# A decode layer's W_down tail loaded in two transfers, with TensorE's loop unrotated and the residual added on VectorE

## The chip, the cores and the metric

The kernel runs on one core of one Trainium2 chip. The metric is device time in microseconds (us), from launch to the last byte written. Engines are named as the profile names them: PE (TensorE; PEld is its weight load), DVE (VectorE), ACT (ScalarE), POOL (GpSimd), SP (SyncE, which issues nearly all transfers here). A trailing q (SPq, DVEq) is the engine's instruction queue.

## The reference

One decode step of a transformer layer for two sequences of one token each. Layernorm, attention over a cache of 8192 positions with 32 heads of 128, a residual, and then a gated feed-forward block with a residual:

```python
q = (layernorm(x) @ wq) -> [b, 32, 1, 128]
p = softmax(q . k_cache * 128**-0.5)          # 8192 positions for each (b, head)
h = x + (p . v_cache) @ wo
d = layernorm(h)
gate, up = d @ W_gate, d @ W_up               # 512 -> 1376
y = h + ((gate * (gate > 0)) * up) @ W_down   # 1376 -> 512
```

All inputs are bfloat16. K and V are 134 MB each, so nearly all of the 281 MB that are read is the cache.

## The kernel before

**Tiles.** The 64 combinations of sequence and head are taken as 32 pairs (`NP`), two heads of one sequence to a pair. A pair has one K tile and one V tile of 128 partitions x 128 positions x 128, 4 MB each. Four buffers `slot[0..3]` take them in turn: even pairs use slots 0 (K) and 1 (V), odd pairs slots 2 and 3. SP issues all loads in one queue, in the order K of pair p + 2, then V of pair p + 2 (`load`, L170; L704 to L711), and waits before each until the slot is free: before K until DVE has multiplied the old tile and PE has transposed it (`kf`), before V until PE's PV product of the old tile is done (token `pv`).

**Scores.** Of the 128 positions of each partition, 96 (`JC`) are scored on DVE: multiply by q (`k_mult`, L553), four halving adds (`k_add`, L558), and a reduce of the last 8 (`k_reduce`, L569). The other 32 are scored on PE in `k_part` (L354): transposes through PSUM (L383), ACT copies them out (`evac`, L581), score products (L366). ACT takes the exponentials of both parts (`exp_pe`, `exp_dve`, L508) into `e_t`, with row sums into `zs`.

**PV and what follows.** `pv` (L394) multiplies the exponentials with V: 32 products of 512 columns (L407) add up in PSUM bank `Op[0]`, over two pairs, which make one group g of two heads for both sequences. `sums` (L583) copies the bank to `os_sb`, `collect` (L420) adds its strips into `Ob`, `z_sum` (L433) adds up the row sums, DVE normalises (L516, L519) and scales (`o_scale`, L523). `o_spread` (L528) places the result in `O_l`, `o_gather` (L436) turns it into columns for the product with wo.

**The loops.** Fifteen iterations (`NI`) of two pairs each run as hardware loops on PE (L444), ACT (L622) and DVE (L588); POOL and SP run straight. PE's loop is rotated by one PV: an iteration does `z_sum`, `k_part` of the even pair, PV of the odd pair of the iteration before, `collect`, PV of the even pair, `k_part` of the odd pair, `o_gather` (L445 to L453). The PV of the odd pair stands behind the transposes of the next pair's K. In the first iteration it runs over a slot that holds wq, with exponentials of zero; so `slot_sem[3]` is raised by hand (L341), `zs` is filled with a pattern of ones (L207), and V of pair 1 is loaded only behind that product (L701 to L703).

**The tail.** Pairs 62 (`P0`) and 63 (`P1`) are written out behind the loops. PE (L465 to L488): `z_sum`, `k_part` of 62, PV of 61, `collect`, `o_gather`, the product with the first 30 heads of wo (L476, 30 products), its collection (L482), `k_part` of 63, PV of 62, PV of 63 in two parts, each with its own transfer and semaphore (L487). DVE (L650 to L663): for pair 62 multiply, first add, then wait for `collect` of pair 61 (`t_ob_loop`), normalise, `o_spread`, the other adds and the reduce; then pair 63. SP (L712 to L727) loads V 63 in two parts, and into slot 0, once K 62 has been used, W_up, W_gate and the first 1280 rows of W_down in blocks of 4, 4 and 2 row groups; the last 96 rows go to `wd_last` in one transfer (L727).

**The feed-forward block.** h is gathered in `hb` (L750); its mean is taken off into `d_b` (L757). PE does 44 products with W_up (L777, `ffn_in`), then 16 small products that add h itself into `Op[0]` (L788, the residual), then two for the variance (L803), then 44 with W_gate. DVE takes the inverse variance `r2` for all 128 partitions (L809, L811), multiplies the up part with it into `u_sb` (L814), and forms `hd` = max(gate, 0) * `u_sb` (L820). The W_down products (L829) add to the residual in `Op[0]`, each block behind its semaphore `sem_wd[k]`; the copy at L835 rounds the sum, and two transfers (L839) write it out.

Of the kernel before, what the change touches and what calls it, by code (L numbers as in the profile page):

```python
# [39 lines left out]
def bass_sequential_preLN__gqa_block_cached__glu_gated_reglu__decode_kernel(  # L40
# [33 lines left out]
    WD_BLOCKS = ((0, 4), (4, 4), (8, 2))  # L74

    with ExitStack() as es:
# [22 lines left out]
        sem_wd = [S(f"wd{i}") for i in range(4)]  # L99
# [42 lines left out]
        ve = sb("ve", [128, B], F32)  # L142
        r2 = sb("r2", [128, B], F32)
# [22 lines left out]
        if True:  # L166

            def program():
# [36 lines left out]
                pool.run(nc.gpsimd.memset(zs[:], 0.0))  # L205
                pool.last()
                for a in range(2):  # L207
                    t_const = pool.run(nc.gpsimd.memset(zs[64 * a:64 * a + 64, a:4:2, :], 1.0))
                    pool.last()
# [92 lines left out]
                t_sel = dve.run(nc.vector.tensor_copy(out=rows[:, DR:], in_=rows[:, 0:DR]))  # L302
                nc.sync.dma_start(
# [37 lines left out]
                nc.tensor.sem_inc(slot_sem[3], 16)  # L341
# [52 lines left out]
                def pv(T, p, parts, between=None, done=None):  # L394
                    s = (2 * p + 1) % 4
                    v_t = tile(s)
                    q = p % PG
                    n = 0
                    for j0, j1, waits in parts:
                        if between and n:  # L400
                            nc.tensor.wait_ge(*waits[0])
                            between()
                        for sem, val in waits:
                            nc.tensor.wait_ge(sem, val)
                        for j in range(j0, j1, VJ):
                            c = 32 * (n % 4)
                            i = nc.tensor.matmul(  # L407
                                Op[0][c:c + 16, :], lhsT=e_t[q][:, j // VJ, :],
                                rhs=v_t[:, j:j + VJ, :].rearrange("p j d -> p (j d)"),
                                start=(q == 0 and n < 4), stop=(q == PG - 1 and n >= J // VJ - 4),  # L410
                                skip_group_check=True)
                            if T is body and n == q == 0:
                                T.mark(("fp", p), i)
                            n += 1
                    if done:
                        i.then_inc(done, 1)
                    else:
                        T.mark(("pv", p), i)

                def collect(T, a, done=None):  # L420
                    nc.tensor.wait_ge(a2p, a)
                    for jj in range(VJ):
                        i = nc.tensor.matmul(  # L423
                            Ob[:, 0:4], lhsT=os_sb[:, jj * Dh:(jj + 1) * Dh],
                            rhs=sel[:, 4 * jj:4 * jj + 4], start=(jj == 0), stop=(jj == VJ - 1))
                        if done and jj == 0:
                            T.mark(done, i)
                    if T is body:
                        i.then_inc(p2d, 1)
                    else:  # L430
                        T.mark("ob", i)
# [12 lines left out]
                with nc.Fori(0, NI, engines=OrderedEngineSet([nc.tensor.engine])):  # L444
                    nc.tensor.wait_ge(a2p, 1)  # L445
                    z_sum(Ob)
                    k_part(body, 0, (2, 3, 4, 5), ((k2p, 1),))
                    pv(body, 1, ((JC, J, ((slot_sem[3], 16),)), (0, JC, ())), done=p2a)
                    collect(body, 7, ("pv", 1))
                    pv(body, 0, ((JC, J, ((slot_sem[1], 16), (a2p, 6))), (0, JC, ((a2p, 8),))))  # L450
                    k_part(body, 1, (9, 10, 11, 12), ((k2p, 2),))
                    nc.tensor.wait_ge(l2p, 1)
                    o_gather(body)  # L453
                    nc.tensor.wait_ge(a2p, EV)
                    nc.tensor.sem_inc(l2p, -1)
                    nc.tensor.sem_inc(slot_sem[1], -16)
                    nc.tensor.sem_inc(slot_sem[3], -16)
                    nc.tensor.sem_inc(k2p, -2)
                    nc.tensor.sem_inc(a2p, -EV)
# [5 lines left out]
                nc.tensor.wait_ge(a2p, 1)  # L465
                z_sum(Ob)
                k_part(tail, P0, (2, 3, 4, 5), ((k2p, 1),))
                pv(tail, P0 - 1, ((JC, J, ((slot_sem[3], 16),)), (0, JC, ())))
                collect(tail, 7)
                t_ob_loop = (pe.sem, tail.at["ob"])  # L470
                nc.tensor.wait_ge(l2p, 1)
                o_gather(tail)
                nc.tensor.wait_ge(a2p, 8)
# [11 lines left out]
                k_part(tail, P1, (11, 12, 13, 14), ((k2p, 2),))  # L485
                pv(tail, P0, ((JC, J, ((slot_sem[1], 16), (a2p, 10))), (0, JC, ())))
                pv(tail, P1, ((V_LAST, J, ((sem_vl[0], 16), (a2p, 16))), (0, V_LAST, ((a2p, 16), (sem_vl[1], 16)))),  # L487
# [8 lines left out]
                def tokp(kind, p, *g):  # L496
                    return tok(kind if kind == "og" else (kind, p) + g, (p + (kind == "pv")) // 2)
# [59 lines left out]
                def k_add(w, run):  # L557
                    run(nc.vector.tensor_tensor(  # L558
                        out=prod[:, 0:JC, 0:w], in0=prod[:, 0:JC, 0:w], in1=prod[:, 0:JC, w:2 * w], op=ALU.add))

                def k_adds(p, run, last, w=Dh):
                    while w > 8:
                        w //= 2
                        last()
                        k_add(w, run)
                    last()
# [54 lines left out]
                nc.scalar.sem_inc(a2p, 1)  # L621
                with nc.Fori(0, NI, engines=OrderedEngineSet([nc.scalar.engine])):  # L622
                    n_a = 0
                    for q in range(PG):
# [7 lines left out]
                        if q == 0:  # L632
                            n_a += 1
                            nc.scalar.wait_ge(p2a, n_a)
                            sums()
# [9 lines left out]
                for p in range(NP):  # L645
# [4 lines left out]
                    if p >= P0:  # L650
# [5 lines left out]
                        dve.last()  # L656
                        k_add(Dh // 2, dve.run)
# [4 lines left out]
                        k_adds(p, dve.run, dve.last, Dh // 2)  # L662
                        t_s[p] = dve.run(k_reduce(p))  # L663
# [20 lines left out]
                    if p == P0:  # L684
                        evacs()
                        act.wait(tokp("pv", p - 1))
                        sums()
                        act.wait(tok("og", NI))
                        to_pe(nc.scalar.activation(
                            out=O_all[:].rearrange("p r b -> p b r"),  # L690
                            in_=Op[1][:, 0:B * DR].rearrange("p (b r) -> p b r", r=DR), func=ACT.Copy))
                        act.wait(tok("op", NI))
                        to_pe(nc.scalar.activation(out=os_sb[:], in_=Op[1][:], func=ACT.Copy))
                        act.wait(t_s[p])
                        exp_dve(p)
# [5 lines left out]
                    if p == 0:  # L701
                        sp.wait(tok(("pv", 1), 0))
                        load(3, A_v_cache, 1)  # L703
# [13 lines left out]
                    if p == NP - 2:  # L717
# [9 lines left out]
                        nc.sync.dma_start(wd_last[:], B_W_down[F - FR:]).then_inc(sem_wd[3], 16)  # L727
# [7 lines left out]
                collect(tail, 17)  # L735
# [50 lines left out]
                for k in range(4):  # L786
                    for c in range(DC):
                        nc.tensor.matmul(  # L788
                            Op[0][32 * k:32 * k + B, c:128:DC], lhsT=hb[:, c * B:(c + 1) * B],
                            rhs=ident[:, 32 * k:32 * k + 32], start=(c == 0), stop=False, skip_group_check=True)  # L790
# [10 lines left out]
                pe.wait(t_vh)  # L801
                for k in range(2):
                    i = nc.tensor.matmul(Sp[0][:, 32:32 + B], lhsT=onesn[:], rhs=vh[:, k * B:(k + 1) * B],  # L803
                                         start=(k == 0), stop=(k == 1))
                t_var = pe.run(i)
                pe.wait((sem_w[1], 16))
                t_g = ffn_in(Op[1], wgt, 0, FC)
                dve.wait(t_var)
                dve.run(nc.vector.tensor_scalar_add(out=ve[:], in0=Sp[0][:, 32:32 + B], scalar1=eps))  # L809
                dve.last()  # L810
                dve.run(nc.vector.reciprocal(out=r2[:], in_=ve[:]))  # L811
                dve.last()
                dve.wait(t_u)
                dve.run(nc.vector.tensor_tensor(  # L814
                    out=u_sb[:].rearrange("p (f b) -> p f b", b=B),
                    in0=Sp[1][:, 0:FC * B].rearrange("p (f b) -> p f b", b=B),
                    in1=r2[:].unsqueeze(1).broadcast_to([128, FC, B]), op=ALU.mult))
# [4 lines left out]
                    in1=u_sb[:], op0=ALU.max, op1=ALU.mult))  # L822
                pe.wait(t_hd)
                order = [(f, k) for k, (r0, n) in enumerate(WD_BLOCKS) for f in range(r0, r0 + n)] + [(10, 3)]
                for n, (f, k) in enumerate(order):
                    pe.wait((sem_wd[k], 16))
                    kp = 128 if f < 10 else FR
                    for m in range(4):
# [3 lines left out]
                            start=False, stop=(n == FC - 1), skip_group_check=True)  # L832
                t_y = pe.run(i)
                dve.wait(t_y)
                t = dve.run(nc.vector.tensor_copy(out=o_r, in_=Op[0][:, 0:128]))  # L835
# [38 lines left out]
```

## Time and profile before

| | |
|---|---|
| median of three runs | 662.96 us (662.75 to 663.32) |
| time of the profiled execution | 662.96 us |
| its span, first to last instruction | 661.7 us, so 1.26 around it |
| busy: PE, PEld | 322.2, 193.9 us (49%, 29%) |
| busy: DVE | 469.1 us (71%) |
| busy: ACT, POOL | 213.8, 74.0 us (32%, 11%) |
| moved | 281.17 MB, mean 425 GB/s |
| DVE's longest wait in sum, for K tiles | 141.6 us in 29 waits |
| PE's longest wait in sum, for ACT's exponentials before `z_sum` | 143.6 us in 15 waits |
| mean granted TensorE clock | 0.594 of full speed |

The profile is of one execution. Its page gives busy times, moved bytes in 40 slices of 16.5 us, the chain of work that ended last (followed back from the last instruction), and the costliest groups of instructions. The trace answers for single stretches: the timeline lists instructions in order with start, duration, engine, line and, in brackets, the idle time before them and what ended it; equal neighbours are merged (x8), and matmuls overlap, so a group's time is from its first start to its last end. Time to landing of a transfer counts from its issue. An idle engine costs nothing where another sets the end.

### The profile page before, as it was taken

To read this page: it belongs to the slowest core of one execution; us is meant where nothing else is said; L and a number is where in the kernel's file an instruction comes from. 1 tells how busy PE (TensorE), PEld (TensorE's weight loads), DVE (VectorE), ACT (ScalarE), POOL (GpSimd) and SP (SyncE) were. 2 spreads that over 40 slices of the span, in tenths; PEclk is the share of its full clock that TensorE was granted. 3 is DMA by queue.
4 is the path that set the end of the run, shared out by engine and by line. 5 is a ranking of instruction groups with operands and counts; after the bars stand their busy time and mean duration, and the time that the engine had idled before them with its cause. 6 is when DMAs were issued, how large, how long until landed. Compare 5 with 4: busy or idle time off the path is not lost.

```text
span 661.7 us, 7610 instructions
## 1 busy us (share of the span) xinstructions
PE 322.2 (49%) x3101; PEld 193.9 (29%) x3101; DVE 469.1 (71%) x279; ACT 213.8 (32%) x431; POOL 74.0 (11%) x127
## 2 busy tenths in 40 slices
PE   2760562616455262644517344451736436174777
PEld 0330342214332121423313233321324223142445
DVE  1585576778767678876767877676787767688891
ACT  1622232233343224334322333432334332232330
POOL 3002002020200202020020202002020200202000
PEclk9875555665557566565755575575555756555665
DMA  9999999999999999999999999999999999999995
GB/s 376 431 430 437 430 430 440 422 436 434 424 438 430 432 438 424 436 434 424 438 430 432 436 426 434 434 426 438 430 432 436 424 434 438 424 436 430 433 416 229
DMA packets 10653, 281.17 MB, mean 425 GB/s; under 512 B 1202, under 2 KB 1300, under 8 KB 1812
## 3 DMA queue, kind: packets, MB, share of 16 engines
q1 hardware_dynamic: 10632, 281.06, 98.9%
q8 instruction: 5, 0.08, 0.1%
q14 instruction: 4, 0.03, 0.0%
q10 hardware_dynamic: 12, 0.00, 0.0%
HBM read 281.05 MB, written 0.00 MB: 425 GB/s over the span
## 4 chain that ended last, share of the span: by engine, by line
DMA 76%; DVE 19%; PE 3%; ACT 1%; issue 1%; SPq 0%; DVEq 0%; ACTq 0%
DMA slot<-in_A_k_cache_dram 76%; DVE prod L553 16%; DVE prod L558 3%; PE O L407 1%; PE Ob L423 0%; DVE scores L569 0%; PE T L383 0%; ACT kT L581 0%; PE S L777 0%; PE O L777 0%; PE O L829 0%; ACT e L508 0%; ACT os_sb L584 0%; SPq L171 0%; PE S L366 0%
## 5 line engine op out<-in xcount | busy, mean ns | idle before, releaser
L553 DVE TENSOR_TENSOR prod<-slot,q_c 128x12288 bf16<-128x12288 bf16 x32 | 209.9, 6559 | 148.3 <-DMA slot<-in_A_k_cache_dram 141.6
L558 DVE TENSOR_TENSOR prod<-prod 128x6144 bf16<-128x6144 bf16 (+3 forms) x128 | 212.2, 1658 | 7.8
L581 ACT ACTIVATE kT<-T 128x1024 bf16<-128x1024 bf16 x128 | 126.4, 1022 | 148.1 <-PE T L383 145.1
L383 PE MATMUL T<-ident_f,slot 128*128 128x128 f32 x512 | 117.2, 387 | 66.3 <-DVEq L602 66.3
L407 PE MATMUL O<-slot,e 128*16 128x512 bf16 x1056 | 115.3, 600 | 59.0 <-ACT e L508 58.8
L383 PEld LDWEIGHTS T<-ident_f,slot 128*128 128x128 f32 x512 | 85.3, 200 | 81.3 <-DVEq L602 80.5
L508 ACT ACTIVATE e<-scores 64x96 bf16<-64x96 f32 x64 | 19.5, 304 | 202.4 <-DVEq L616 196.6
L434 PE MATMUL Ob<-zs,ones_f 128*128 128x8 f32 x32 | 9.3, 364 | 143.6 <-ACT e L508 143.6
L550 POOL COPY q_c<-q_all 128x136 bf16<-128x136 bf16 x32 | 57.4, 1794 | 195.1 <-DVEq L606 165.0
L366 PE MATMUL S<-q_c,kT 128*128 128x4 bf16 x1024 | 47.8, 169 | 37.6 <-ACT kT L581 37.0
L407 PEld LDWEIGHTS O<-slot,e 128*16 128x16 bf16 x1056 | 29.4, 117 | 116.5 <-ACT e L508 65.6
L366 PEld LDWEIGHTS S<-q_c,kT 128*128 128x128 bf16 x1024 | 40.4, 105 | 65.5 <-ACT kT L581 64.1
L434 PEld LDWEIGHTS Ob<-zs,ones_f 128*128 128x128 f32 x32 | 7.8, 304 | 145.2 <-ACT e L508 145.1
L533 POOL MEMSET O_l<- 128x40 bf16 (+1 forms) x13 | 1.8, 136 | 304.0 <-DVEq L613 304.0
L569 DVE TENSOR_REDUCE scores<-prod 128x96 f32<-128x768 bf16 x32 | 30.5, 953 | 2.8
L423 PEld LDWEIGHTS Ob<-sel,os_sb 128*128 128x128 f32 x136 | 23.0, 255 | 26.2 <-ACT os_sb L584 26.2
L423 PE MATMUL Ob<-sel,os_sb 128*128 128x4 f32 x136 | 24.4, 303 | 11.9 <-ACT os_sb L584 11.9
L584 ACT ACTIVATE os_sb<-O 128x512 f32<-128x512 f32 x17 | 10.1, 597 | 45.0 <-PE O L407 45.0
L581 ACT ACT_TABLE_LOAD x15 | 19.2, 1283 | 0.3
L508 ACT ACTIVATE e<-S 64x32 bf16<-64x32 f32 x64 | 12.9, 202 | 15.2 <-PE S L366 14.8
L508 ACT ACTIVATION_READ_ACCUMULATOR e<-S 64x1 f32 x64 | 12.8, 201 | 0.7
L508 ACT ACTIVATION_READ_ACCUMULATOR e<-scores 64x1 f32 x64 | 11.8, 184 | 0.0
(104 smaller groups left out, 87.8 us busy)
## 6 DMA issues: line engine op xcount, KB each, us to landing
slot<-in_A_k_cache_dram SPq DMA_DIRECT2D x32, 4096.0 KB, 30.8
slot<-in_A_v_cache_dram SPq DMA_DIRECT2D x31, 4096.0 KB, 29.6
slot<-in_A_wq_dram SPq DMA_DIRECT2D x1, 4096.0 KB, 12.2
X<-in_A_wo_dram SPq DMA_DIRECT2D x1, 3840.0 KB, 50.3
slot<-in_A_v_cache_dram SPq DMA_DIRECT2D x1, 3072.0 KB, 20.5
slot<-in_B_W_up_dram SPq DMA_DIRECT2D x1, 1376.0 KB, 25.5
slot<-in_B_W_gate_dram SPq DMA_DIRECT2D x1, 1376.0 KB, 28.4
slot<-in_A_v_cache_dram SPq DMA_DIRECT2D x1, 1024.0 KB, 22.6
```

What stands on the lines that cost most here:

```text
L366: i = nc.tensor.matmul(Sp[p % 2][:, 2 * jj:2 * jj + 4], lhsT=kv_[:, k, r, :], rhs=q_c[p % 2][:, 4 * r:4 * r + 4], start=(r == 0), stop=(r ...
L383: i = nc.tensor.transpose(Tp[g % 2][:, k * 128:(k + 1) * 128], k_t[:, j:j + 2, :].rearrange("p j d -> p (j d)").bitcast(F32), ident_f[:])
L407: i = nc.tensor.matmul(Op[0][c:c + 16, :], lhsT=e_t[q][:, j // VJ, :], rhs=v_t[:, j:j + VJ, :].rearrange("p j d -> p (j d)"), start=(q == ...
L423: i = nc.tensor.matmul(Ob[:, 0:4], lhsT=os_sb[:, jj * Dh:(jj + 1) * Dh], rhs=sel[:, 4 * jj:4 * jj + 4], start=(jj == 0), stop=(jj == VJ - 1))
L434: return nc.tensor.matmul(bank[:, ZC:ZC + 8], lhsT=ones_f[:], rhs=zs[:], start=True, stop=True)
L508: i = nc.scalar.activation(out=e_t[q][h, j0 // VJ:j1 // VJ, 8 * q:8 * q + 8].rearrange("p g (j a) -> p g j a", a=2)[:, :, :, a], in_=src(h ...
L550: nc.gpsimd.tensor_copy(out=q_c[p % 2][:], in_=q_all[:, p]).then_inc(g2d, 1)
L553: return nc.vector.tensor_tensor(out=prod[:, 0:JC, :], in0=tile((2 * p) % 4)[:, 0:JC, :], in1=q_c[p % 2][:, 8:QW].unsqueeze(1).broadcast_t ...
L558: run(nc.vector.tensor_tensor(out=prod[:, 0:JC, 0:w], in0=prod[:, 0:JC, 0:w], in1=prod[:, 0:JC, w:2 * w], op=ALU.add))
L569: return nc.vector.tensor_reduce(out=scores[p % PG][:, 0:JC], in_=prod[:, 0:JC, 0:8], axis=AX.X, op=ALU.add)
L581: to_pe(nc.scalar.activation(out=kT[gg % 2][:], in_=Tp[gg % 2][:].bitcast(BF16), func=ACT.Copy))
L584: to_pe(nc.scalar.activation(out=os_sb[:], in_=Op[0][:], func=ACT.Copy))
```

## The change

- PE's loop is no longer rotated. An iteration does `k_part` of the even pair, `collect` of the group before, PV of the even pair, `k_part` of the odd pair, `o_gather`, PV of the odd pair (behind its own exponentials), `z_sum`. The dummy product of the first iteration goes, with the raised semaphore, the pattern of ones and ACT's extra increment of `a2p`; ACT no longer waits ahead of `sums` in the loop.
- V of pair 1 is loaded behind the q projection, ahead of `X` (wo), in place of behind the dummy product.
- In the tail, `collect` of pair 61 comes ahead of `k_part` of 62, and DVE normalises that group behind the reduce of pair 62 in place of behind its first add. ACT does `sums` ahead of the tail's first copies, and `exp_dve` of 62 ahead of the second copy to `os_sb`.
- The residual is no longer added in PSUM. The 16 products go to `Tp[0]`, DVE copies them to `h_r`, and the last instruction on DVE is `Op[0] * r2 + h_r` in place of the copy. The inverse variance comes off `u_sb` (now a plain copy) and is made per output row: two variance products ahead of W_gate become eight small ones behind it.
- The last 96 rows of W_down load as 68 and 28 rows with a semaphore each; the last product waits for both.

The diff, cut to its core:

```diff
+    WD_TAIL = ((0, 68), (68, 28))
...
-                for a in range(2):
-                    t_const = pool.run(nc.gpsimd.memset(zs[64 * a:64 * a + 64, a:4:2, :], 1.0))
-                    pool.last()
+                t_const = pool.run(nc.gpsimd.memset(zs[:], 0.0))
...
+                sp.wait(t_q)
+                load(3, A_v_cache, 1)
                 nc.sync.dma_start(
                     X[:], A_wo[0:128 * DR].rearrange("(p r) n -> p (r n)", r=DR)).then_inc(sem_wo, 16)
...
-                nc.tensor.sem_inc(slot_sem[3], 16)
...
                 with nc.Fori(0, NI, engines=OrderedEngineSet([nc.tensor.engine])):
-                    nc.tensor.wait_ge(a2p, 1)
-                    z_sum(Ob)
-                    k_part(body, 0, (2, 3, 4, 5), ((k2p, 1),))
-                    pv(body, 1, ((JC, J, ((slot_sem[3], 16),)), (0, JC, ())), done=p2a)
-                    collect(body, 7, ("pv", 1))
-                    pv(body, 0, ((JC, J, ((slot_sem[1], 16), (a2p, 6))), (0, JC, ((a2p, 8),))))
-                    k_part(body, 1, (9, 10, 11, 12), ((k2p, 2),))
+                    k_part(body, 0, (1, 2, 3, 4), ((k2p, 1),))
+                    collect(body, 6)
+                    pv(body, 0, ((JC, J, ((slot_sem[1], 16), (a2p, 5))), (0, JC, ((a2p, 7),))))
+                    k_part(body, 1, (8, 9, 10, 11), ((k2p, 2),))
                     nc.tensor.wait_ge(l2p, 1)
                     o_gather(body)
-                    nc.tensor.wait_ge(a2p, EV)
                     nc.tensor.sem_inc(l2p, -1)
+                    pv(body, 1, ((JC, J, ((slot_sem[3], 16), (a2p, 12))), (0, JC, ((a2p, EV),))))
+                    z_sum(Ob)
...
-                nc.tensor.wait_ge(a2p, 1)
-                z_sum(Ob)
+                collect(tail, 1)
+                t_ob_loop = (pe.sem, tail.at["ob"])
                 k_part(tail, P0, (2, 3, 4, 5), ((k2p, 1),))
-                pv(tail, P0 - 1, ((JC, J, ((slot_sem[3], 16),)), (0, JC, ())))
-                collect(tail, 7)
-                t_ob_loop = (pe.sem, tail.at["ob"])
...
                         t_dm[p] = dve.run(k_mult(p))
-                        dve.last()
-                        k_add(Dh // 2, dve.run)
+                        k_adds(p, dve.run, dve.last)
+                        if p == P0:
+                            dve.wait(tokp("pv", p - 2))
+                        t_s[p] = dve.run(k_reduce(p))
                         if p == P0:
                             dve.wait(t_ob_loop)
                             normalize(Ob, dve.run, dve.last)
                             o_spread(g - 1, dve, dve.run(o_scale()))
-                        k_adds(p, dve.run, dve.last, Dh // 2)
-                        t_s[p] = dve.run(k_reduce(p))
...
-                    if p == 0:
-                        sp.wait(tok(("pv", 1), 0))
-                        load(3, A_v_cache, 1)
...
-                        nc.sync.dma_start(wd_last[:], B_W_down[F - FR:]).then_inc(sem_wd[3], 16)
+                        for k, (r0, n) in enumerate(WD_TAIL):
+                            nc.sync.dma_start(
+                                wd_last[r0:r0 + n], B_W_down[F - FR + r0:F - FR + r0 + n]).then_inc(sem_wd[3 + k], 16)
...
-                        nc.tensor.matmul(
-                            Op[0][32 * k:32 * k + B, c:128:DC], lhsT=hb[:, c * B:(c + 1) * B],
-                            rhs=ident[:, 32 * k:32 * k + 32], start=(c == 0), stop=False, skip_group_check=True)
+                        i = nc.tensor.matmul(
+                            Tp[0][32 * k:32 * k + B, c:128:DC], lhsT=hb[:, c * B:(c + 1) * B],
+                            rhs=ident[:, 32 * k:32 * k + 32], start=True, stop=True)
+                t_hr = pe.run(i)
+                pe.wait((sem_w[1], 16))
+                t_g = ffn_in(Op[1], wgt, 0, FC)
...
+                pe.wait(t_vh)
+                for m in range(4):
+                    for k in range(2):
+                        i = nc.tensor.matmul(Sp[0][32 * m:32 * m + B, 32:33], lhsT=vh[:, k * B:(k + 1) * B],
+                                             rhs=onesn[:, 0:1], start=(k == 0), stop=(k == 1))
...
-                    pe.wait((sem_wd[k], 16))
+                    pe.wait((sem_wd[k], 16), (sem_wd[max(k, 2 * k - 2)], 16))
...
-                t = dve.run(nc.vector.tensor_copy(out=o_r, in_=Op[0][:, 0:128]))
+                t = dve.run(nc.vector.scalar_tensor_tensor(
+                    out=o_r, in0=Op[0][:, 0:128], scalar=r2[:, 0:1], in1=h_r, op0=ALU.mult, op1=ALU.add))
```

## The prediction

> **What bounds the kernel now.** I read the page from the transfers inwards: the moved bytes per slice, the share of the queue, then the chain that ended last.
>
> ```profile
> GB/s 376 431 430 437 430 430 440 422 436 434 424 438 430 432 438 424 436 434 424 438 430 432 436 426 434 434 426 438 430 432 436 424 434 438 424 436 430 433 416 229
> ...
> q1 hardware_dynamic: 10632, 281.06, 98.9%
> ...
> DMA 76%; DVE 19%; PE 3%; ACT 1%; issue 1%; SPq 0%; DVEq 0%; ACTq 0%
> ```
>
> One queue moves 281 MB at 430 GB/s without a gap, until the last slice. The chain is a transfer of K for 76% of the span, so for 600 us nothing but the transfers counts. DVE rests 4 to 5 us ahead of most K tiles (141.6 us in 29 waits). An edit can gain only behind the last K tiles, or lose by starving the queue.
>
> So I read the end. First VectorE:
>
> ```profile
> 604.34 6.73 DVE L558 TENSOR_TENSOR prod<-prod 128x6144 bf16<-128x6144 bf16 x4
> ...
> 612.98 6.56 DVE L553 TENSOR_TENSOR prod<-slot,q_c 128x12288 bf16<-128x12288 bf16 x1 [0.92 <-DVEq L618]
> 619.57 3.36 DVE L558 TENSOR_TENSOR prod<-prod 128x6144 bf16<-128x6144 bf16 x1
> 624.89 0.17 DVE L516 TENSOR_REDUCE zr<-Ob 128x4 f32<-128x8 f32 x1 [1.96 <-PE Ob L423]
> ...
> 630.36 6.56 DVE L553 TENSOR_TENSOR prod<-slot,q_c 128x12288 bf16<-128x12288 bf16 x1
> ```
>
> From 597.6 on DVE works through K 61, 62 and 63 with no wait on a transfer. K 63 was issued at 604.28 and landed 22.4 later, at 626.7, but its multiply starts at 630.36. Between them lies a wait of 1.96 us for `Ob`: the collect of pair 61, which stands behind the rotated PV. Now TensorE:
>
> ```profile
> 623.80 1.05 PE L423 MATMUL Ob<-sel,os_sb 128*128 128x4 f32 x8 [0.71 <-ACT os_sb L584]
> 626.14 0.26 PE L439 MATMUL O<-rsel,O_l 128*128 128x30 bf16 x4 [1.29 <-DVE O_l L539]
> 626.74 3.37 PE L476 MATMUL O<-X,O_all 128*2 128x512 bf16 x30 [0.33 <-ACT O_all L689]
> ...
> 638.36 3.59 PE L407 MATMUL O<-slot,e 128*16 128x512 bf16 x32
> 645.61 2.74 PE L407 MATMUL O<-slot,e 128*16 128x512 bf16 x24 [3.65 <-ACT e L508]
> ...
> 648.80 1.03 PE L407 MATMUL O<-slot,e 128*16 128x512 bf16 x8
> ```
>
> PV 62 ends at 641.95, and PV 63 waits 3.65 us for DVE's scores. From there everything to the end is one chain. Last, the transfers behind it, with issue times and the time to landing:
>
> ```profile
> 624.46 0.43 SPq L720 DMA_DIRECT2D slot<-in_B_W_gate_dram  x1
> 624.94 1.38 SPq L724 DMA_DIRECT2D slot<-in_B_W_down_dram  x3
> 626.36 4.54 SPq L727 DMA_DIRECT2D wd_last<-in_B_W_down_dram  x1
> ```
>
> ```profile
> slot<-in_B_W_gate_dram SPq DMA_DIRECT2D x1, 1376.0 KB, 28.4
> ...
> slot<-in_B_W_down_dram SPq DMA_DIRECT2D x1, 256.0 KB, 30.3
> wd_last<-in_B_W_down_dram SPq DMA_DIRECT2D x1, 96.0 KB, 30.0
> ```
>
> W_gate lands at 652.9, the third W_down block (issued near 625.9) at 656.2, `wd_last` at 656.4. The compute uses them at 656.0, near 658.85 and at 659.0: the transfers lead by 3.1 and 2.6 us. That is all a shorter compute chain can win.
>
> **The change, part by part.** The sum goes against the profiled execution: span 661.7, time 662.96, so 1.26 around the span; its time is also the median of the three runs.
>
> 1. *Loop without rotation, steady state.* The same instructions in another order, less one dummy PV. PV of an odd pair now waits in line for that pair's scores. By DVE's rows these are ready 14.4 us after K lands (6.6 + 6.7 + 1.0); exponentials 0.8, the last 24 PV matmuls 2.74, z_sum 0.6: TensorE is free 18.6 us after landing, and K tiles land 19.44 apart (multiplies at 578.19 and 597.64). The odd V slot frees about 12 us earlier than now. Now V 5 is issued at 122.55 and lands 18.3 later, of which 9.7 is its own, so 8 us were still queued; after the change about 20. The transfers cover this: I take 0. Without cover, each us of starving would count 15 times.
>
> 2. *V 1 ahead of X on SP.* SP now waits for the q projection (ends 16.65) before V 1 and X. Queued then are K 0, V 0, K 1, landing until 44.4, so 0; K 2 stays behind both. It bounds what is queued behind the wait: 28 us of cover.
>
> 3. *The tail on DVE.* Collect of pair 61 moves ahead of K 62's transposes. PV 61 ends near 612.96 + 2.74 = 615.7; copy and collect end by 619.1, long before DVE asks. DVE: 612.98 + 14.31 (630.36 to 644.67 in this trace) = 627.3, normalise and spread 1.20 (624.89 to 626.09), K 63 from 628.5 instead of 630.36. Scores of 63 after ACT: 645.47 - 1.86 = 643.6; the first part of V 63 lands at 623.14 + 20.5 = 643.6 as well.
>
> 4. *The tail on TensorE.* The spread now ends at 628.5 instead of 626.09, 2.4 later, since it stands behind the whole of K 62. All that waits on it moves too: gather, 30 wo products, K 63's transposes, PV 62, which ends at 641.95 + 2.4 = 644.4. PV 63 begins there: 644.4 for 645.61, a gain of 1.2, not 1.9. TensorE has taken DVE's place.
>
> 5. *The clock.* PV 62 and PV 63 now run without a gap, over 6 us of dense work. What this clock does is in the rows:
>
> ```profile
> 389.73 1.90 PE L407 MATMUL O<-slot,e 128*16 128x512 bf16 x32
> ```
>
> ```profile
> 626.40:629.70 3.30, 2.97 (x31) 0.91 (x30) 3.20 (x4) 0.24 (x1) 0.00 (x0) 0.50 1.04 447
> 629.80:633.10 3.30, 2.61 (x18) 2.30 (x13) 3.27 (x2) 1.34 (x5) 0.00 (x0) 1.00 1.02 432
> ...
> 645.60:649.80 4.20, 4.20 (x34) 1.34 (x34) 0.34 (x2) 0.00 (x0) 0.00 (x0) 0.50 1.03 431
> ```
>
> These are stretches of the span with the engines' busy times; the third number from the right is the granted clock. After 3.3 us of wo products it went from 0.50 to 1.00, while the 4.2 us of PV 63 alone did not raise it: from 650 to 660 it stood at 0.50. At 1.00 a PV takes 1.90 for 3.59, a collect 1.05 for 1.87 (623.80 against 650.53). Bounds: from no raise (0) to a raise at the head of PV 63 (half of 4.2, plus 0.8: 2.9). I take about 1.5 to 2.5, the upper half, since the stretch is twice as long as the one that raised it.
>
> The Trainium skill, "TensorE: Matmul & The Clock Gate", Part 1, says that the gate looks at free-running windows of 3.41 us and opens after a busy one. By it any stretch of 6.8 us holds a whole window, and the raise would be sure here; PV 61 (3.59 us, then 1.00 from 623) agrees, and PV 62 (3.59 us, no raise) is the same rule with another phase.
>
> 6. *FFN.* The two variance products ahead of W_gate go (0.14). Eight small ones come behind it, 0.2 us by the 16 residual products (0.41), inside the 0.35 us in which TensorE waits for `hd`; without that cover 0.2. The residual copy (near 0.29, as L835) lies under W_gate's 1.7. The last CAST of 0.29 becomes a scale-and-add on the same 128 x 128; I add 0.05, bounds 0 and 0.3 (a second pass like it). ve and r2 (0.33) hide under the W_down products (1.3).
>
> 7. *W_down's tail as 68 and 28 rows.* One more issue; SP has nothing else to do. The 96 rows land 0.2 after the block before. Bounds: 0.3 earlier, if the last engine to finish carries none of it, to 2.6 later, if 68 KB ran at a sixteenth of 430 GB/s on one engine. I take 0, by the nearest row.
>
> The Trainium skill, "DMA: Bandwidth & Descriptors", "Why a DMA increments its semaphore by 16 and not by 1", speaks against this edit: the number of engines is the largest divisor up to 16 of the row count, 16 for 96, 4 for 68, 14 for 28. By its figure each of four engines moves 17 KB in place of 6, an estimated 0.4 us more; no row here shows it.
>
> *Sum.* Parts 3 to 6 ask for 1.2 + 0.14 - 0.05 = 1.3 without the clock and 2.8 to 3.8 with it. Block 3 of W_down at 656.2 and the tail at 656.4 stop it: the products now need 0.55 from there (658.85 to 659.40), so they end near 656.85, 2.55 earlier, and with the 0.05 the span is 659.2. Time: 659.2 + 1.26 = 660.5.
>
> **Rivals.**
> - *A, forecast:* the end is set by W_down's landing, 660.5 (659.6 to 661.1, by landings 0.6 either side, which is the spread of the three runs). For it: dense PV 62 and 63. Chance 0.62.
> - *B, no raise of the clock* or a gap between the PVs: only 1.3 gained, 661.65 (661.2 to 662.3). For it: 645.60 to 649.80 stayed at 0.50. Chance 0.18.
> - *C, the gain doesn't arrive:* the tail transfers land 2.6 later, at 659.0: four products 0.45 and 2.3 to the end give a span of 661.75, time 663.0. Chance 0.07.
> - *D, slower:* TensorE's loop turn. Now it is hidden under waits of 9.0 us ahead of z_sum; after the change the last one stands between PV 61 and K 62's transposes. It costs between nothing and those 9 us; DVE's exit shows 0.92, which I take. TensorE would be through K 62 at 616.3 + x + 1.9 + 5.9 and is first needed at 628.5, so x is free to 4.4; from 7 on the kernel is slower by more than 0.2%, and at 9 PV 63 starts at 649.0, time 666.2 without a raise. Chance 0.13.
>
> **How the numbers follow.** A measurement of this kernel tells about 0.2%, 1.3 us, from no change. A is faster; B lies on that edge, and I give half to each side; C is within it; D is slower. Faster 0.70, same 0.17, slower 0.13. The range takes A and B: 659.6 to 662.3, and leaves out 0.2.
>
> **What would show it.** DVE's `zr` of pair 61 with no wait and K 63's multiply near 628.5; PV 62 and 63 adjacent, near 641 to 648; granted clock 1.00 within them; the last W_down products waiting for a transfer near 656.2; K still starting about every 19.44 us. Wrong if DVE's waits for K vanish from the loop (starved or late slots), if PV 63 still waits for `e`, or if the tail lands past 657.

## The result, and the profile after

| | before | after |
|---|---|---|
| median, 6 runs each on one chip | 662.75 us (661.43 to 663.32) | 660.33 us (660.24 to 660.74) |
| ratio | | 0.9968 (95%: 0.9955 to 0.9981) |
| time of the profiled execution | 662.96 us | 660.33 us |
| its span | 661.7 us | 659.0 us |

After is faster, by 2.4 us; 660.5 was forecast. One later run of after took 687.45 us at a mean clock of 1.00; it is the only one of its kind, and no median or ratio here counts it. One correction to the names ahead: `NP` is 32, so the last three pairs are 29, 30 and 31 in the code. The text ahead, and the expectations, call them 61, 62 and 63. These names are kept here, so that the parts can be laid beside each other; no time depends on them.

The page first: moved bytes of the last slices are now 419 and 299 GB/s (416 and 229 before), and this is the queue and the chain:

```profile
q1 hardware_dynamic: 10634, 281.06, 99.3%
...
DMA 80%; DVE 18%; issue 1%; PE 1%; SPq 0%; DVEq 0%
DMA slot<-in_A_k_cache_dram 76%; DVE prod L541 16%; DMA slot<-in_B_W_gate_dram 4%; DVE prod L550 2%; PE O L759 0%; PE O L811 0%; DVE scores L555 0%; SPq L173 0%; DVEq L588 0%; DVEq L592 0%; SPq L176 0%; SPq L177 0%; DVE kT L818 0%; DVE hd L
```

The queue's share rose by 0.4 points, as 2.7 us of tail are gone and the bytes are the same. PE's share of the chain fell from 3% to 1%, and a transfer that was not in it before, W_gate, has 4%: the end now hangs on a landing. The timeline of DVE after, start and duration first:

```profile
613.02 6.56 DVE L541 TENSOR_TENSOR prod<-slot,q_c 128x12288 bf16<-128x12288 bf16 x1 [0.92 <-DVEq L604]
619.61 6.73 DVE L550 TENSOR_TENSOR prod<-prod 128x6144 bf16<-128x6144 bf16 x4
626.38 0.95 DVE L555 TENSOR_REDUCE scores<-prod 128x96 f32<-128x768 bf16 x1
627.25 0.16 DVE L504 TENSOR_REDUCE zr<-Ob 128x4 f32<-128x8 f32 x1
...
628.35 6.55 DVE L541 TENSOR_TENSOR prod<-slot,q_c 128x12288 bf16<-128x12288 bf16 x1
```

`zr` of pair 61 has no bracket, so it waits for nothing; before it waited 1.96 us. K 63 is multiplied 2.0 us earlier. TensorE after:

```profile
617.04 3.20 PE L406 MATMUL O<-slot,e 128*16 128x512 bf16 x32 [13.78 <-DMA slot<-in_A_v_cache_dram]
...
620.95 1.05 PE L418 MATMUL Ob<-sel,os_sb 128*128 128x4 f32 x8 [0.39 <-ACT os_sb L570]
...
626.49 0.37 PE L365 MATMUL S<-q_c,kT 128*128 128x4 bf16 x8 [0.56 <-ACT kT L567]
628.49 0.29 PE L432 MATMUL O<-rsel,O_l 128*128 128x30 bf16 x4 [1.63 <-DVE O_l L527]
...
640.92 4.50 PE L406 MATMUL O<-slot,e 128*16 128x512 bf16 x56
...
646.36 0.61 PE L406 MATMUL O<-slot,e 128*16 128x512 bf16 x8 [0.62 <-DMA slot<-in_A_v_cache_dram]
...
652.91 1.72 PE L759 MATMUL O<-d_b,slot 128*128 128x2 bf16 x44 [0.60 <-DMA slot<-in_B_W_gate_dram]
```

PV 62 (32 products) and the 24 products of PV 63 are one group of 56 now, without the 3.65 us of before, and they take 4.50 us; at the 3.59 and 2.74 of before they would take 6.33. Behind them two brackets name transfers, V 63's last part and then W_gate. A third transfer is waited for within the W_down products; the list of waits has it (sum in us, number, longest):

```profile
PEld O L811 <- DMA slot<-in_B_W_down_dram: 0.5, 2, 0.3
```

The engines' busy times by stretch show the clock, third number from the right, after:

```profile
640.90:643.60 2.70, 2.70 (x32) 0.99 (x32) 1.69 (x3) 1.56 (x8) 0.00 (x0) 0.50 0.95 399
643.60:647.00 3.40, 2.75 (x46) 1.01 (x34) 0.35 (x2) 0.00 (x0) 0.00 (x0) 1.00 1.01 423
647.00:650.40 3.40, 1.89 (x24) 1.64 (x25) 0.66 (x4) 0.60 (x1) 0.00 (x0) 1.00 1.00 421
```

It went to 1.00 in the middle of the 56 products and stayed there through the collect (1.05 us). Before, the same three stretches stood at 0.50.

### The profile page after: what moved, and what is told of

Its sections match the earlier page's. It is cut to its first block, busy times and chain, and to the rows that moved or that the text cites. A ratio compares the mean times of both kernels' runs of the same rounds, so it can differ in the third digit from the quotient of the medians.

```text
span 659.0 us, 7584 instructions
## 1 busy us (share of the span) xinstructions
PE 322.5 (49%) x3073; PEld 187.6 (28%) x3073; DVE 469.3 (71%) x280; ACT 213.7 (32%) x431; POOL 73.6 (11%) x125
## 4 chain that ended last, share of the span: by engine, by line
DMA 80%; DVE 18%; issue 1%; PE 1%; SPq 0%; DVEq 0%
DMA slot<-in_A_k_cache_dram 76%; DVE prod L541 16%; DMA slot<-in_B_W_gate_dram 4%; DVE prod L550 2%; PE O L759 0%; PE O L811 0%; DVE scores L555 0%; SPq L173 0%; DVEq L588 0%; DVEq L592 0%; SPq L176 0%; SPq L177 0%; DVE kT L818 0%; DVE hd L792 0%; DVEq L604 0%
## 5 line engine op out<-in xcount | busy, mean ns | idle before, releaser
L541 DVE TENSOR_TENSOR prod<-slot,q_c 128x12288 bf16<-128x12288 bf16 x32 | 209.9, 6559 | 148.2 <-DMA slot<-in_A_k_cache_dram 141.6
L406 PE MATMUL O<-slot,e 128*16 128x512 bf16 x1024 | 117.6, 613 | 220.4 <-ACT e L496 146.5
L382 PE MATMUL T<-ident_f,slot 128*128 128x128 f32 x512 | 108.0, 364 | 29.0 <-DVEq L588 29.0
L406 PEld LDWEIGHTS O<-slot,e 128*16 128x16 bf16 x1024 | 26.3, 112 | 286.4 <-ACT e L496 173.1
L382 PEld LDWEIGHTS T<-ident_f,slot 128*128 128x128 f32 x512 | 78.6, 187 | 44.0 <-DVEq L588 43.2
L365 PEld LDWEIGHTS S<-q_c,kT 128*128 128x128 bf16 x1024 | 38.9, 103 | 67.9 <-ACT kT L567 66.8
L418 PE MATMUL Ob<-sel,os_sb 128*128 128x4 f32 x136 | 30.2, 345 | 24.3 <-ACT os_sb L570 24.3
L418 PEld LDWEIGHTS Ob<-sel,os_sb 128*128 128x128 f32 x136 | 28.7, 312 | 26.2 <-ACT os_sb L570 26.2
L526 POOL COPY rsel<-rows 128x30 bf16<-128x30 bf16 x28 | 5.9, 209 | 33.3 <-DVEq L599 32.5
```

What stands on the lines that cost most here:

```text
L365: i = nc.tensor.matmul(Sp[p % 2][:, 2 * jj:2 * jj + 4], lhsT=kv_[:, k, r, :], rhs=q_c[p % 2][:, 4 * r:4 * r + 4], start=(r == 0), stop=(r ...
L382: i = nc.tensor.transpose(Tp[g % 2][:, k * 128:(k + 1) * 128], k_t[:, j:j + 2, :].rearrange("p j d -> p (j d)").bitcast(F32), ident_f[:])
L406: i = nc.tensor.matmul(Op[0][c:c + 16, :], lhsT=e_t[q][:, j // VJ, :], rhs=v_t[:, j:j + VJ, :].rearrange("p j d -> p (j d)"), start=(q == ...
L418: i = nc.tensor.matmul(Ob[:, 0:4], lhsT=os_sb[:, jj * Dh:(jj + 1) * Dh], rhs=sel[:, 4 * jj:4 * jj + 4], start=(jj == 0), stop=(jj == VJ - 1))
L541: return nc.vector.tensor_tensor(out=prod[:, 0:JC, :], in0=tile((2 * p) % 4)[:, 0:JC, :], in1=q_c[p % 2][:, 8:QW].unsqueeze(1).broadcast_t ...
```

## The experiments

Each of the change's four parts could have brought the gain: the loop, DVE's moved block, the FFN, the split transfer. The theory is that the moved block alone does it, in two steps: K 63 starts earlier, and the two PVs close up, which raises the clock; what then stops the gain is the landing of the W loads. The rivals: the loop without rotation, or the FFN with the split, brings the gain; or TensorE's own chain ends as late as the landing. Every kernel was timed beside the kernel before on the same chip; ratios are to it.

### The moved block alone

In the kernel before, with its rotated loop, its FFN and its single transfer:

```diff
-                        dve.last()
-                        k_add(Dh // 2, dve.run)
+                        k_adds(p, dve.run, dve.last)
+                        if p == P0:
+                            dve.wait(tokp("pv", p - 2))
+                        t_s[p] = dve.run(k_reduce(p))
                         if p == P0:
                             dve.wait(t_ob_loop)
                             normalize(Ob, dve.run, dve.last)
                             o_spread(g - 1, dve, dve.run(o_scale()))
-                        k_adds(p, dve.run, dve.last, Dh // 2)
-                        t_s[p] = dve.run(k_reduce(p))
```

> The kernel before, with one part of the change alone: in the tail, VectorE normalises the group before the last pairs behind the reduce of the last pair but one, not behind its first add. Loop, feed-forward block and loads are those of before. Theory (the gain is made behind the last K tiles and stopped by W_down's landing): the wait for Ob of 1.96 us goes, the last multiply starts near 628.5 for 630.36, the two last PV products run without a gap, the granted clock rises in them, and the time is about 660.5 (660.2 to 661.2). Rival 1 (the unrotated loop makes the gain): 662.7. Rival 2 (the split transfer or the feed-forward edit makes it): 662.7.

Measured 660.15 us (660.05 to 660.29, 5 runs) beside 663.24: ratio 0.9956 (0.9941 to 0.9971), just under the 660.2 to 661.2 expected. TensorE's timeline of this kernel:

```profile
640.87 4.53 PE L407 MATMUL O<-slot,e 128*16 128x512 bf16 x56
646.30 0.61 PE L407 MATMUL O<-slot,e 128*16 128x512 bf16 x8 [0.57 <-DMA slot<-in_A_v_cache_dram]
```

It is the picture of after, to 0.06 us. So this move alone gives the whole gain, and the loop, the FFN and the split are not needed for it.

### The split and the FFN taken back

After, with the 96 rows in one transfer:

```diff
-    WD_TAIL = ((0, 68), (68, 28))
+    WD_TAIL = ((0, 96),)
...
-                    pe.wait((sem_wd[k], 16), (sem_wd[max(k, 2 * k - 2)], 16))
+                    pe.wait((sem_wd[k], 16))
```

> The changed kernel with one part undone: the last 96 rows of W_down in one transfer with one semaphore. Theory: 660.3 to 660.6, since the block ahead of the tail lands at 656.1 anyway and the tail 0.2 behind it. Rival 2 (the split transfer makes the gain): 662 or more.

Measured 660.50 us (660.36 to 660.93, 5 runs), 0.9962 (0.9947 to 0.9977).

After, with the FFN of before (residual into `Op[0]`, two variance products ahead of W_gate, `r2` for all partitions, the plain copy at the end; the diff is the change's FFN part turned round):

> The changed kernel with one part undone: residual in PSUM, inverse variance on all partitions ahead of the gate, as before. Theory: the 0.14 us of the two variance products come back ahead of W_gate's products, where TensorE waits 0.60 us for W_gate's landing, so they are covered; the last instruction is the copy of 0.29 for 0.35. 660.2 to 660.4. Rival 3 (the feed-forward edit makes the gain): 662 or more.

Measured 660.35 us (660.18 to 660.83, 5 runs), 0.9958 (0.9943 to 0.9973). Both overlap after's 660.24 to 660.74: neither part is worth anything that can be resolved.

### Is it the clock?

In the kernel before, 28 products like those of PV, into a bank nobody reads, fill the gap between PV 62 and PV 63. They bring no result earlier; they add work:

```diff
+                for n in range(28):
+                    nc.tensor.matmul(
+                        Tp[0][32 * (n % 4):32 * (n % 4) + 16, 0:512], lhsT=e_t[0][:, n, :],
+                        rhs=slot[1][:, n * 512:n * 512 + 512], start=True, stop=True)
                 pv(tail, P1, ...
```

> The kernel before, with 28 extra PV products of 512 columns into an unused PSUM bank, placed in the 3.65 us in which TensorE waits between the two last PV products; their results are not used. VectorE's wait of 1.96 us stays. Theory (half of the gain or more is the clock): the granted clock is 1.00 by the last PV product, which takes 2.1 for 4.2, the collect 1.05 for 1.87, and the time falls to 660.4 to 661.2. Rival 4 (the gain is only the 1.2 us by which the PV product starts earlier): no gain, 662.7 or a little more.

Measured 660.63 us (660.09 to 660.90, 6 runs), 0.9964 (0.9952 to 0.9977). The profiled execution, the fastest of the six (660.09):

```profile
640.31 1.88 PE L488 MATMUL T<-slot,e 128*16 128x512 bf16 x28
643.56 1.47 PE L407 MATMUL O<-slot,e 128*16 128x512 bf16 x24 [1.37 <-DMA slot<-in_A_v_cache_dram]
```

The granted clock goes to 1.00 near 640.7, 3.8 us after PV 62 began and 0.4 us into the filler, and the 24 products of PV 63 take 1.47 us for 2.74. In this execution PV 61 also ran at the full clock (1.90 us at 619.11), so DVE did not wait for it there, though the expectation said that it would; that execution alone could not tell the two steps apart. The other five runs took 660.31 to 660.90, while 9 of 68 runs of the kernel before, in the later comparisons, came under 661. The same filler with 16 columns in place of 512 leaves the instructions and takes away their length:

> The kernel before with the same 28 extra products in the same place, but 16 columns wide in place of 512, so that TensorE issues as many instructions and does a thirty-second of the work. Theory (the clock follows dense work): no raise behind them, the last PV product at 0.50 in most executions, and the time stays near that of before, 662 to 663.3. Rival 4 or any effect of the extra instructions themselves: the same 660.6 as with the wide ones.

Measured 663.25 us (661.65 to 663.79, 12 runs), 1.0008 (0.9996 to 1.0021): no gain. Its windows and the group of PV 63:

```profile
643.60:647.00 3.40, 0.90 (x12) 0.38 (x16) 1.51 (x2) 0.74 (x4) 0.00 (x0) 0.50 1.02 424
647.00:650.40 3.40, 3.33 (x30) 0.99 (x22) 0.35 (x2) 0.01 (x1) 0.00 (x0) 0.50 1.00 419
```

```profile
642.44 0.38 PE L488 MATMUL T<-slot,e 128*16 128x16 bf16 x28
646.11 2.74 PE L407 MATMUL O<-slot,e 128*16 128x512 bf16 x24 [3.29 <-ACT e L512]
```

28 instructions that last 0.38 us in sum leave the clock at 0.50 and the wait at 3.29. Work that nobody uses, at full width, made the kernel 0.36% faster; the same number of short instructions did nothing. That is the strongest evidence for the clock as a cause in its own right. What the earlier start of K 63 is worth without the raise was not tried.

### Is the landing the end?

After, without the loads of W_up, W_gate and W_down and the waits for them (left out: the products run over what the slot still holds, the last 96 rows over zeros):

> The changed kernel without the loads of W_up, W_gate and W_down: their products run over what lies in the slot, the last 96 rows over zeros. 4.3 MB (about 10 us of transfers) go from the end of the queue. Theory (W_gate's and W_down's landing set the end): TensorE no longer waits 0.60 for W_gate nor about 0.3 within the W_down products, so the span falls by 0.7 to 1.0 and the time to 659.3 to 659.7, no further, as the chain from V of the last pair stays. Rival 5 (the compute chain alone sets the end): 660.3, unchanged.

Measured 659.99 us (12 runs), 0.9963 (0.9949 to 0.9976), in two groups: six runs at 659.12 to 659.47, five at 660.51 to 660.87, and one at 662.35 whose mean clock over the span was 0.518 (0.575 to 0.632 in the others). So the fall by about 1 us came in half of the runs only (there at or just under the 659.3 to 659.7 expected). With nothing to land, the other half ends where after ends. The profiled execution, of the later group, shows why:

```profile
616.93 3.59 PE L407 MATMUL O<-slot,e 128*16 128x512 bf16 x32 [13.81 <-DMA slot<-in_A_v_cache_dram]
642.59 5.05 PE L407 MATMUL O<-slot,e 128*16 128x512 bf16 x56
```

PV 61 waits for V 61, which lands at 616.9, and here it runs at 0.50 (3.59 us). Behind it, in the new order, stand the collect and all of K 62: they end at 629.1, past the spread of 628.3, and PV 62 begins 1.7 later than in after's own profile (640.92). Of the 1.7, 0.5 has passed at the gather (628.99 for 628.49). Another 0.7 comes behind it, where TensorE waits 1.07 for ACT's copy in place of 0.33, as ACT takes K 62's exponentials first. The rest is K 63's transposes at the lower clock. So a second theory was formed: in half of the executions it is the loop's new order that ends last, since V 61 stands ahead of K 62's transposes; the rival was that the clock at the last PV products alone makes the two groups, in any order. The moved block alone, without the W loads, tells them apart, as its rotated loop has K 62 ahead of PV 61:

> The kernel of e1 (before's loop, VectorE's normalise late) without the loads of W_up, W_gate and W_down; products run over what lies in the slot, the last 96 rows over zeros. Asked: why the changed kernel without these loads fell into two groups, 659.1 to 659.5 and 660.5 to 660.9. Theory 7 (in the unrotated loop the PV product of the pair ahead of the tail waits for its V, which lands at 616.9, ahead of K's transposes, so that TensorE reaches its last PV products 1.6 us later whenever the clock is at 0.50 there): with before's loop the transposes come first, so one group, 658.9 to 659.6. Rival 8 (the two groups come from the clock at the last PV products alone): two groups here too, 1.3 to 1.6 apart.

Measured 659.14 us (658.77 to 659.71, 6 runs), 0.995 (0.9933 to 0.9966): one group, though 0.9 wide, and no later one. The theory stands, and the rival, which asked for two groups here too, was not seen. Without the loads W_gate's products start with no wait in this profile, 0.82 ahead of after's 652.91:

```profile
652.09 1.69 PE L767 MATMUL O<-d_b,slot 128*128 128x2 bf16 x44
```

### Where the block may stand in the new loop

After, with DVE's normalise back behind the first add of K 62:

```diff
-                        k_adds(p, dve.run, dve.last)
-                        if p == P0:
-                            dve.wait(tokp("pv", p - 2))
-                        t_s[p] = dve.run(k_reduce(p))
+                        dve.last()
+                        k_add(Dh // 2, dve.run)
                         if p == P0:
                             dve.wait(t_ob_loop)
...
+                        k_adds(p, dve.run, dve.last, Dh // 2)
+                        t_s[p] = dve.run(k_reduce(p))
```

> The changed kernel with one part undone: VectorE normalises the group before the last pairs behind its first add, as before. Loop and tail order on TensorE stay changed. The collect is done near 622, the first add near 623, so there is no wait of note, TensorE gets its columns about 3 us earlier and is done with the last but one PV product before VectorE has the last scores. Theory: 660.1 to 660.6, since W_down's landing still sets the end. Rival 6 (the gain of the changed kernel hangs on the late normalise): 662 or more.

Measured 660.40 us (12 runs, eleven of them 660.24 to 660.66), 0.997 (0.9957 to 0.9983). The twelfth took 662.74 at a mean clock of 0.526. In this kernel's profile `zr` of pair 61 has no bracket (622.66), so the loop's new order removes DVE's wait too: there `collect` comes early enough wherever the block stands. One step of the expectation did not come: the gather is 1.2 us earlier than after's (627.25 for 628.49), not 3, as it stands behind K 62 on TensorE, and the 56 products run without a gap here as well. There are two ways to the same gain, and the change holds both.

After once more, in the same comparison:

> The changed kernel again, beside the runs above on one chip: 660.2 to 660.7, with a smaller spread than the kernel before, because its end is a landing and not a chain whose clock depends on the moment.

Measured 660.50 us (660.19 to 660.83, 11 runs), 0.9972 (0.9958 to 0.9986). Its profiled execution is one with PV 61 at 0.50: PV 62 begins at 642.54, W_gate's products run without a wait, and the last product ends at 656.70 as in after (656.62). In this execution the compute chain ends where the landing would let it: the two tie.

### The better version

The moved block alone seemed a little ahead of after. Both again on one chip, and later on, beside runs of the kernel before of their own, the moved block with the change's FFN and split but with the loop of before:

> The kernel of e1 again, beside the changed kernel on one chip: before's loop, feed-forward block and loads, VectorE's normalise late. Theory 7: as fast as the changed kernel or faster by up to 0.3 us (660.0 to 660.4), since TensorE's order in the tail is not held up by that V. Rival 1 (the unrotated loop has a gain of its own): the changed kernel is faster.

> The changed kernel beside e10 on one chip: 660.2 to 660.6 by theory 7, up to 0.3 us behind e10; ahead of e10 by rival 1.

> The kernel of e1 (before's loop, VectorE's normalise late) with the two other parts of the change added: the residual on VectorE with the variance behind the gate, and the last 96 rows in 68 and 28. Theory: both are covered by W_gate's and W_down's landing, so 660.0 to 660.2, no different from e1 (660.15 and 660.16). Rival 2 or 3 (one of these parts has a gain of its own): 659.9 or less.

| kernel | us | ratio |
|---|---|---|
| moved block alone | 660.16 (659.85 to 660.23, 7 runs) beside 662.85 | 0.996 (0.9945 to 0.9975) |
| after | 660.54 (660.10 to 660.90, 12 runs) beside 662.85 | 0.9969 (0.9957 to 0.9980) |
| moved block, new FFN and split | 660.36 (660.16 to 660.65, 11 runs) beside 662.76 | 0.9967 (0.9953 to 0.998) |

The moved block alone is ahead of after by 0.38 us, with ranges that hardly overlap; that is under the 0.2% named ahead, and rests on the runs of one chip here and on 660.15 in the first comparison. So a few moved lines are as good as the whole change, and perhaps a little better. The FFN and the split add nothing to them: 660.36 was expected at 660.0 to 660.2 and is no better than 660.16. By these medians, from two comparisons, they would cost 0.2 and leave the loop's order the other half of the 0.38; neither can be resolved.

## Why the prediction was right

- **Parts 1 and 2, steady state: right.** K's multiplies after start at 578.25 and 597.67, 19.42 apart (19.45 before), and DVE's waits for K add up to 141.6 us in both kernels. PE's bracket ahead of the collect is 0.39, so the loop's turn, rival D, cost little, and D is out.
- **Part 3, DVE: right, but its figure for PV 61 was wrong.** K 63 came at 628.35, forecast 628.5. PV 61 was put at 2.74 us behind its scores, to end near 615.7. V 61 lands only at 616.9, and all 32 products stand behind it. Rival D's sum used the same figure and gave TensorE 4.4 us to spare behind K 62. PE is through K 62 at 626.9 with the raised clock and at 629.1 without, so the slack was 1.6 or -0.6.
- **Part 4, TensorE: right in its end.** With a slack of 1.6 DVE's spread still sets the gather, as forecast (PV 62 at 640.92; 644.4 - 3.59 = 640.8 was said). With -0.6, PV 62 is 1.7 late. The miss cost nothing in the time, because W_gate and W_down land no earlier: that the landing covers this too was not forecast, and is luck.
- **Part 5, the clock: right.** The raise came in the 56 products. `O_cur` behind the last collect is at 648.83 for 652.51, 3.7 earlier; 1.2 of it was forecast without the clock, and the other 2.5 is the top of the 1.5 to 2.5 taken. The two fillers show that dense work is enough for the gain. The Trainium skill, "TensorE: Matmul & The Clock Gate", Part 1, was drawn on for a raise that is sure in any 6.8 us of dense work, an estimate from its window of 3.41 us. Here 6.3 us at 0.50 would have been a little short of sure, and each profiled execution of a kernel that closes the two PVs up had the raise, in one of them only at the end of the products (the 56 took 6.00 us with the moved block, new FFN and split). Rival B was not seen in a profile. The two runs at 662.35 and 662.74 had a low mean clock over the span (0.518 and 0.526); no profile shows their tails, so they may be B.
- **Part 6, FFN: right.** The eight small products (0.21 us at 654.55) lie under the wait for `hd`; the last instruction takes 0.35 for 0.29. The 0.14 saved ahead of W_gate bought nothing, as TensorE then waits 0.60 for W_gate to land.
- **Part 7, the split: right in the time.** The landing events of the trace show 4 engines for the 68 rows (655.0 to 655.9), 14 for the 28 rows (the last at 656.14) and 16 for the 96 rows of before (the last at 656.38). These are the numbers of engines that the Trainium skill, "DMA: Bandwidth & Descriptors", "Why a DMA increments its semaphore by 16 and not by 1", gives. The 0.4 us worked out from it were not seen: they land by 655.9 and 656.14, with the block ahead of them (656.09). Rival C is out.
- **The sum: right.** Products forecast to end near 656.85, measured 656.62; span 659.2 forecast, 659.0 measured. The sum named W_down's landing as the stop; the trace has two in a row, W_gate's (0.60 at 652.91) and then W_down's (up to 0.3). The gain stops at the landings, as the kernel without W loads shows: 659.14 against 660.16, both with the moved block alone, leaves 1.0 us to them.

What stays open: which window of the clock a tail meets in each execution. The kernel before has it as well: 9 of its 68 runs in the last three comparisons took 660.0 to 660.7, like after, and the rest 661.4 to 664.0; no profile shows one of the nine, so that a raise made them, behind PV 62 or already in PV 61, is likely from the fillers, not shown.

## What to carry to other kernels

Where transfers bound the body, look for the gain behind the last large tile, and ask for each wait removed what is late next; here the landing of the last weights capped it at about 2.5 us. A gap between two dense stretches on TensorE cost twice here, by the wait and by the clock that did not rise, so closing it can be worth more than the wait. When an early product moves ahead of other work in a loop, look at the landing of its own tile, not only at the scores that it waits for.

## What was not expected of the hardware

SP's timeline after, as issued, for the blocks of W_down and the two last transfers of 68 and 28 rows:

```profile
626.31 1.39 SPq L704 DMA_DIRECT2D slot<-in_B_W_down_dram  x3
627.74 13.14 SPq L708 DMA_DIRECT2D wd_last<-in_B_W_down_dram  x2
```

13.14 us for two, where three larger ones of 128 rows took 1.39. The other profiles say that this is a wait. A single transfer of 96 rows was through at 630.6 to 631.0 in all six profiles that have one, whether it began at 624.27 (6.43 us) or at 630.01 (0.87 us). The two of 68 and 28 rows were through at 640.8 to 641.2 in all six with the split, begun at 626.49 (14.36 us) to 630.10 (11.03 us). So the end stays and the start moves; what is waited for is not shown. Nothing was queued behind them on SP, so it cost nothing; with other loads behind them it could.

Also, the 16 engines of a transfer do not finish together. Of the 96 rows before, eleven engines have landed between 654.24 and 655.19 and five follow between 655.78 and 656.38. The V tile of pair 61 shows the same in the middle of the stream: fourteen between 614.81 and 615.66, the last two at 616.88 and 616.95. Both are complete 2.1 us after their first engine.
